# Two-bank PSUM tiles in the attention stages and a new sharing of the split steps in an attention and two-MLP kernel

## The chip, the cores and the metric

One core of one Trainium2 chip runs the whole program in one launch. The metric is the device time in microseconds (us) of one execution; a kernel's time is the median of several executions. The engines are TensorE (PE; PEld is its weight load), VectorE (DVE), ScalarE (ACT), GpSimd (POOL) and SyncE (SP), which issues most DMAs. Each runs its own instructions strictly in the order of its queue, and they wait for one another by semaphores.

## The reference, cut to what matters

For 4 batches of 12 heads with 448 positions of 64 elements:

```python
rmsnorm(x, g) = x / sqrt(mean(x*x) + 1e-6) * g
scores = (1/8) * rmsnorm(q, g_q) @ rmsnorm(k, g_k).T
attn   = exp(scores - max(scores)); attn /= sum(attn) + 1e-9
x = (attn @ v), heads side by side          # 1792 x 768
x = relu(x @ w_in)**2 @ w_out               # 768 -> 2048 -> 768
h = (x @ w1) * (x @ w2) @ w3                # 768 -> 1024 -> 1024
out = h @ wo2                               # 1024 -> 768
```

The MLP weights come as 64-bit floats, the rest as 32-bit floats.

## The kernel before, in words

**Precision.** TensorE works on fp32r operands. To keep fp32 accuracy each operand is cut into a high part (a rounded copy) and a low part (the value less the high part), and a product is three matmuls: high x high (L258), high weight x low activation (L259) and low weight x high activation (L260), the helper `mm3`.

**Weights.** They come in units of 128 x 384 or 128 x 512 (`units`), used in a fixed order. Units 0 to 31 are w3 and wo2, from which the kernel first makes w3 @ wo2 (`gen_w3o`, the stage called w3o below, U0 = 32). Units 32 to 119 are the MLP weights of batch 0 (U1 = 120). For both the 64-bit words are turned into fp32 on the chip: `words` (L192 on ACT for the high word, L195 on ACT or L197 on POOL for the low word, chosen by `LOW_ENG`), `join` (L204 on DVE), `split_hi` (L104 on ACT), `split_lo` (L112, on POOL or DVE by `LO0_ENG`). In the MLP of batch 0 the fp32 words are also stored; the batches 1 to 3 load those and only split them, with the low part always on POOL. There are four buffers each for the 64-bit unit (`raw64`), for the fp32 unit (`raw`) and for the split one (`hl`); the load of a unit is issued five units ahead, its words come three ahead, its join two and its high part one.

**Attention.** Heads run in a loop. Each head has stages: `head_prep` (k and q split; the high part of q, `qh`, at L487 on ACT or L489, by `QHI_ENG` with one letter for each batch), `stage_k` (k transposed, bank `kv`), `stage_qk` twice (two blocks of 112 rows each: L520 and L521 make scores in PSUM tile `sc`, L522 their negated maximum, L523 scales it), `stage_exp` (L538, two exponentials with sums), `stage_t` four times (L560 transposes the probabilities into PSUM tile `pt`, ACT copies it as the high part, `stage_lo` subtracts on DVE for the low part), `stage_v` (L609 into `kv`, then ACT and L617 add the halves into `xf`), and every second head `stage_x` (L598 transposes the inverse sums into `kv`, L623 multiplies `xf`, then it is split as the MLP's input).

**Order.** Between the stages `fill(n)` puts a share of the MLP matmuls of the batch before (of w3o in the first 12 heads). What the program gives is not quite the order on an engine: a planner lists the instructions of each engine beforehand by program order and by when it expects the operands, so matmuls of the fill can stand between those of a stage. PSUM has 8 banks: two `sc`, two `pt`, one `kv`, three `mm` for the fill.

Of the kernel before, what the change touches and what calls it, by code (L numbers as in the profile page):

```python
# [8 lines left out]
F32 = mybir.dt.float32  # L9
F32R = mybir.dt.float32r  # L10
# [4 lines left out]
ALU = mybir.AluOpType  # L15
AX = mybir.AxisListType
# [13 lines left out]
def attention_moe_kernel(  # L30
# [56 lines left out]
    t3 = ctx.enter_context(tc.tile_pool(name="t3", bufs=3))  # L87
    small = ctx.enter_context(tc.tile_pool(name="small", bufs=4))
    dram = ctx.enter_context(tc.tile_pool(name="dram", bufs=1, space=bass.MemoryType.DRAM))
    ps_sc = ctx.enter_context(tc.tile_pool(name="ps_sc", bufs=2, space=bass.MemoryType.PSUM))  # L90
    ps_pt = ctx.enter_context(tc.tile_pool(name="ps_pt", bufs=2, space=bass.MemoryType.PSUM))
    ps_kv = ctx.enter_context(tc.tile_pool(name="ps_kv", bufs=1, space=bass.MemoryType.PSUM))
    ps_mm = ctx.enter_context(tc.tile_pool(name="ps_mm", bufs=3, space=bass.MemoryType.PSUM))

# [221 lines left out]
    def gen_moe(b):  # L316
# [4 lines left out]
        for half in range(2):  # L321
            g = []

            def relu2(ps):
                r = t2.tile([128, S], F32, name="r", tag="r")
                nc.scalar.activation(out=r, in_=ps, func=AF.Relu)
                t = actp.tile([128, 2, S], F32R, name="act", tag="act")
                gf = t2.tile([128, S], F32, name="gf", tag="gf")
                nc.scalar.activation(out=t[:, 0, :], in_=r, func=AF.Square)
                nc.vector.tensor_tensor(out=gf, in0=ps, in1=r, op=ALU.mult)  # L330
                sub_on("g", t[:, 1, :], gf, t[:, 0, :].bitcast(F32))
                g.append(t)

            def keep(e):
# [174 lines left out]
    def stage_qk(h, s):  # L509
        if not (0 <= h < NH):  # L510
            return
        d = heads[h]
        nb = d["nb"] = small.tile([P, 2], F32, name="nb", tag="nb")
        c0 = 2 * s
        o = d["sc"] = [None, None]
        for j in range(2):
            c = c0 + j
            ps = ps_sc.tile([128, 512], F32, name="sc", tag="sc")
            o[j] = ps[:P, :S]
            nc.tensor.matmul(o[j], d["qh"][:, c * P:(c + 1) * P], d["kt"], start=True, stop=False)  # L520
            nc.tensor.matmul(o[j], d["ql"][:, c * P:(c + 1) * P], d["kt"], start=False, stop=True)  # L521
            nc.vector.tensor_reduce(out=nb[:, j:j + 1], in_=o[j], axis=AX.X, op=ALU.max, negate=True)  # L522
        nc.vector.tensor_tensor(out=nb, in0=nb, in1=d["rq"][:, c0:c0 + 2], op=ALU.mult)  # L523

    def stage_exp(h, s):
# [24 lines left out]
            )  # L550
            sums2[h // 2] = wide.rearrange("p c i d -> p c (i d)")

    def stage_t(h, kc):
        if not (0 <= h < NH):
            return
        d = heads[h]
        k0, kn = KCS[kc]
        ps = ps_pt.tile([128, 512], F32, name="pt", tag="pt")
        for c in range(C):
            nc.tensor.transpose(ps[:kn, c * P:(c + 1) * P], d["p"][c][:, k0:k0 + kn], ident)  # L560
        if kn == 128:
            t = t3.tile([128, 2, S], F32R, name="ptr", tag="ptr", bufs=3)
            hi, lo = t[:, 0, :], t[:, 1, :]
            d["pt"][kc] = [hi, lo]
        else:
            t = t1.tile([128, S], F32R, name="pte", tag="pte")
            hi, lo = t[:kn, :], t[kn:, :]
            d["pt"][kc] = [t]
        copy_on("a", hi, ps[:kn, :S])
        d["lo"].append((lo, ps[:kn, :S], hi.bitcast(F32)))  # L570
# [92 lines left out]
    for h in range(NH + 1):  # L663
# [91 lines left out]
```

## Time and profile before

| | us |
|---|---|
| median of 3 executions | 1255.01 (1254.23 to 1256.89) |
| the profiled execution | 1256.72 |
| its span, first to last instruction | 1254.9 |
| TensorE busy | 1176.6 |
| POOL busy | 788.5 |
| ACT busy | 749.0 |
| DVE busy | 692.6 |

The mean granted TensorE clock is 0.984 of full speed. Busy times are sums over the whole span; matmuls overlap one another in the record, so a busy TensorE need not be one at its peak. The stages differ: the attention of batch 0 with w3o comes first, then three batches of attention with the MLP of the batch before, and the last MLP alone.

### The profile page before, as it was taken

What the parts mean: (1) busy time and instruction counts of PE and PEld (TensorE: products, weight loads), DVE (VectorE), ACT (ScalarE), POOL (GpSimd) and SP (SyncE); (2) the same over time, 40 slices, a digit from 0 to 9 for tenths busy, and PEclk for the clock granted to TensorE, in tenths of its full rate; (3) what the DMA queues carried; (4) which work ended last, traced back from release to release, by engine and by line L of the source; (5) the groups of instructions that cost most, each with busy time, mean ns of one, the idle gap of its engine ahead of it and who ended that gap; (6) DMA issues with size and microseconds to landing.
All of it is one profiled execution on the core that took longest, in us unless ns stands there. A gap on an engine that the chain in (4) does not pass through costs nothing.

```text
span 1254.9 us, 18695 instructions
## 1 busy us (share of the span) xinstructions
PE 1176.6 (94%) x6192; PEld 1063.9 (85%) x6192; DVE 692.6 (55%) x1274; ACT 749.0 (60%) x1595; POOL 788.5 (63%) x770
## 2 busy tenths in 40 slices
PE   3789999798888999999999999999999999999998
PEld 2578888687777889999999998999999999999998
DVE  6699877666668676556557546555664431012100
ACT  5788877776755665665655555655545554443342
POOL 5874427746765555675876664765765656768773
PEclk9899999998998989999999999999999999999999
DMA  7774447866866754433334344333433333433342
GB/s 211 243 222 135 150 143 205 260 199 192 257 171 200 229 154 143 123 111 115 114 92 124 96 130 137 96 105 86 117 89 88 92 106 110 120 104 111 101 122 94
DMA packets 102129, 178.71 MB, mean 142 GB/s; under 512 B 11056, under 2 KB 65552, under 8 KB 102032
## 3 DMA queue, kind: packets, MB, share of 16 engines
q1 hardware_dynamic: 98576, 172.01, 46.9%
q10 hardware_dynamic: 3456, 5.51, 1.2%
q8 instruction: 49, 0.80, 0.3%
q14 instruction: 48, 0.39, 0.1%
HBM read 149.95 MB, written 27.53 MB: 141 GB/s over the span
## 4 chain that ended last, share of the span: by engine, by line
PE 65%; DVE 5%; DMA 4%; POOL 3%; ACT 2%; issue 2%; SPq 0%; POOLq 0%; DVEq 0%; ACTq 0%
PE mm L258 18%; PE mm L259 18%; PE mm L260 18%; PE pt L560 3%; PE kv L609 3%; DMA raw<-w 2%; DVE raw L204 2%; POOL hl L112 2%; PE sc L520 2%; PE sc L521 2%; DMA raw<-w_in 1%; DVE nb L522 1%; PE kv L504 1%; PE kv L598 1%; ACT p L538 0%
## 5 line engine op out<-in xcount | busy, mean ns | idle before, releaser
L112 POOL TENSOR_TENSOR hl<-raw,hl 128x384 fp32r<-128x384 f32 (+1 forms) x395 | 459.3, 1166 | 270.3 <-ACT hl L104 266.8
L104 ACT ACTIVATE hl<-raw 128x384 fp32r<-128x384 f32 (+1 forms) x416 | 234.0, 564 | 147.2 <-PE mm L260 79.3
L259 PE MATMUL mm<-x,hl 128*128 128x448 f32 (+1 forms) x832 | 307.3, 369 | 7.8 <-POOL x L112 7.8
L258 PE MATMUL mm<-x,hl 128*128 128x448 f32 (+1 forms) x832 | 311.9, 375 | 2.8 <-ACT x L104 1.8
L260 PE MATMUL mm<-x,hl 128*128 128x448 f32 (+1 forms) x832 | 306.3, 368 | 2.0 <-POOL hl L112 1.2
L258 PE MATMUL mm<-act,hl 128*128 128x448 f32 (+1 forms) x640 | 239.0, 373 | 0.0
L259 PE MATMUL mm<-act,hl 128*128 128x448 f32 (+1 forms) x640 | 235.7, 368 | 3.0 <-POOL act L112 2.9
L260 PE MATMUL mm<-act,hl 128*128 128x448 f32 (+1 forms) x640 | 234.6, 367 | 1.6 <-DVE hl L112 1.4
L538 ACT ACTIVATE p<-sc,nb,rr 112x448 f32<-112x448 f32 x192 | 137.5, 720 | 82.3 <-DVE nb L523 81.8
L259 PEld LDWEIGHTS mm<-x,hl 128*128 128x128 f32 x832 | 158.9, 191 | 21.7 <-POOL x L112 9.5
L258 PEld LDWEIGHTS mm<-x,hl 128*128 128x128 f32 x832 | 158.8, 191 | 17.4 <-ACT x L104 3.2
L260 PEld LDWEIGHTS mm<-x,hl 128*128 128x128 f32 x832 | 158.7, 191 | 16.3 <-POOL hl L112 2.3
L204 DVE SCALAR_TENSOR_TENSOR raw<-raw 128x384 uint32<-128x384 uint32 (+1 forms) x120 | 94.9, 794 | 77.0 <-POOL hl L112 66.3
L259 PEld LDWEIGHTS mm<-act,hl 128*128 128x128 f32 x640 | 121.9, 191 | 14.2 <-POOL act L112 4.6
L522 DVE TENSOR_REDUCE nb<-sc 112x1 f32<-112x448 f32 x192 | 113.3, 616 | 35.3 <-PE sc L521 34.0
L260 PEld LDWEIGHTS mm<-act,hl 128*128 128x128 f32 x640 | 121.8, 190 | 11.9 <-DVE hl L112 1.8
L112 POOL TENSOR_TENSOR act<-gf,act 128x448 fp32r<-128x448 f32 x96 | 117.5, 1225 | 22.0 <-DVE gf L330 8.5
L258 PEld LDWEIGHTS mm<-act,hl 128*128 128x128 f32 x640 | 122.2, 191 | 9.4
L112 DVE TENSOR_TENSOR ptr<-pt,ptr 128x448 fp32r<-128x448 f32 x144 | 86.8, 618 | 72.2 <-ACT ptr L104 72.0
L560 PE MATMUL pt<-ident,p 112*128 112x112 f32 (+1 forms) x768 | 101.0, 269 | 13.1 <-DVE ptr L112 10.3
L192 ACT ACTIVATE raw<-raw 128x384 f32<-128x384 f32 (+1 forms) x120 | 71.4, 598 | 57.9 <-DMA raw<-w 25.5
L560 PEld LDWEIGHTS pt<-ident,p 112*128 112x128 f32 (+1 forms) x768 | 82.5, 138 | 20.4 <-DVE ptr L112 10.9
(76 smaller groups left out, 1517.5 us busy)
## 6 DMA issues: line engine op xcount, KB each, us to landing
raw<-f_in SPq DMA_DIRECT2D x96, 192.0 KB, 2.4
raw<-f_out SPq DMA_DIRECT2D x72, 256.0 KB, 2.6
raw<-f SPq DMA_DIRECT2D x96, 192.0 KB, 2.4
raw<-w_in SPq DMA_DIRECT2D x32, 384.0 KB, 3.5
raw<-w_out SPq DMA_DIRECT2D x24, 512.0 KB, 4.2
raw<-w SPq DMA_DIRECT2D x32, 384.0 KB, 3.8
raw<-w3o SPq DMA_DIRECT2D x48, 256.0 KB, 2.7
qt<-q_t SPq DMA_DIRECT2D x48, 224.0 KB, 2.8
```

The source lines that it names most:

```text
L104: nc.scalar.activation(out=out, in_=in_, func=AF.Copy)
L112: e.tensor_tensor(out=out, in0=in0, in1=in1, op=ALU.subtract)
L192: nc.scalar.activation(out=hi, in_=hi, func=AF.Prelu, scale=2.0**-112, alpha=-(2.0**32))
L204: nc.vector.scalar_tensor_tensor(out=f[:, :n].bitcast(U32), in0=t[:, :n, 1], scalar=3, in1=t[:, :n, 0], op0=ALU.logical_shift_left, op1=AL ...
L258: nc.tensor.matmul(ps, w[:, 0, wk, :], x[0], start=(i == 0), stop=False)
L259: nc.tensor.matmul(ps, w[:, 0, wk, :], x[1], start=False, stop=False)
L260: nc.tensor.matmul(ps, w[:, 1, wk, :], x[0], start=False, stop=(i == last))
L520: nc.tensor.matmul(o[j], d["qh"][:, c * P:(c + 1) * P], d["kt"], start=True, stop=False)
L522: nc.vector.tensor_reduce(out=nb[:, j:j + 1], in_=o[j], axis=AX.X, op=ALU.max, negate=True)
L538: nc.scalar.activation(out=p, in_=o[j], func=AF.Exp, scale=d["rq"][:, c:c + 1], bias=nb[:, j:j + 1], accum_out=sm[:, i, c:c + 1],)
L560: nc.tensor.transpose(ps[:kn, c * P:(c + 1) * P], d["p"][c][:, k0:k0 + kn], ident)
L609: nc.tensor.matmul(ps[:, :S], w, m, start=(n == 0), stop=(n == len(ops) - 1))
```

## The change

1. **Scores.** `ps_sc` holds one tile of two banks in place of two tiles of one bank. Both blocks of a stage go into it, and one maximum over both banks replaces two.
2. **Transposes.** `ps_pt` holds one tile of two banks. `stage_t` runs twice for each head in place of four times: half 0 makes the first two key blocks (one copy and one subtraction over both banks), half 1 the third and the short fourth (a copy and a subtraction for each). The SBUF tile for the first two is one tile.
3. **Inverse sums.** `norms_to_rows` takes its bank from `ps_mm` (three) and not from `ps_kv` (one).
4. **Sharing.** The low words of units 0 to 31 are all on POOL (before, each third on ACT). The low parts of units 0 to 31 are all on POOL (before, each fifth on DVE); those of units 32 to 119 are on DVE for each third unit (before, each fifth). `qh` of the first 12 heads goes from ACT to POOL. In the MLP of batch 0 the subtraction after the squared relu goes from POOL to DVE (16 of them).

```diff
-    LO0_ENG = "ggggv"
+    LO0_ENG = "ggv"
-    QHI_ENG = "aavv"
+    QHI_ENG = "gavv"
-    ps_sc = ctx.enter_context(tc.tile_pool(name="ps_sc", bufs=2, space=bass.MemoryType.PSUM))
-    ps_pt = ctx.enter_context(tc.tile_pool(name="ps_pt", bufs=2, space=bass.MemoryType.PSUM))
+    ps_sc = ctx.enter_context(tc.tile_pool(name="ps_sc", bufs=1, space=bass.MemoryType.PSUM))
+    ps_pt = ctx.enter_context(tc.tile_pool(name="ps_pt", bufs=1, space=bass.MemoryType.PSUM))
-        if LOW_ENG[i % len(LOW_ENG)] == "a":
+        if i >= U0 and LOW_ENG[i % len(LOW_ENG)] == "a":
-        sub_on(LO0_ENG[i % len(LO0_ENG)] if i < U1 else "g", t[:, 1, :n], raws.pop(i)[:, :n], ...)
+        sub_on(LO0_ENG[i % len(LO0_ENG)] if U0 <= i < U1 else "g", t[:, 1, :n], raws.pop(i)[:, :n], ...)
-                sub_on("g", t[:, 1, :], gf, t[:, 0, :].bitcast(F32))
+                sub_on("g" if b else "v", t[:, 1, :], gf, t[:, 0, :].bitcast(F32))
 # stage_qk
+        ps = ps_sc.tile([128, 2, 512], F32, name="sc", tag="sc")
+        o = d["sc"] = [ps[:P, j, :S] for j in range(2)]
         for j in range(2):
...
-            nc.vector.tensor_reduce(out=nb[:, j:j + 1], in_=o[j], axis=AX.X, op=ALU.max, negate=True)
+        nc.vector.tensor_reduce(out=nb, in_=ps[:P, :, :S], axis=AX.X, op=ALU.max, negate=True)
 # stage_t(h, half)
+        ps = ps_pt.tile([128, 2, 512], F32, name="pt", tag="pt")
+        for j in range(2):
+            k0, kn = KCS[2 * half + j]
+            for c in range(C):
+                nc.tensor.transpose(ps[:kn, j, c * P:(c + 1) * P], d["p"][c][:, k0:k0 + kn], ident)
+        if half == 0:
+            t = t3.tile([128, 2, 2, S], F32R, name="ptr", tag="ptr0", bufs=1)
...
+            parts = [(t[:, 0], t[:, 1], ps[:, :, :S])]
+        else:
...
+            parts = [(t[:, 0, :], t[:, 1, :], ps[:, 0, :S]), (e[:kn, :], e[kn:, :], ps[:kn, 1, :S])]
+        for hi, lo, x in parts:
+            copy_on("a", hi, x)
+            d["lo"].append((lo, x, hi.bitcast(F32)))
 # norms_to_rows
-        ps = ps_kv.tile([128, 512], F32, name="kv", tag="kv")
+        ps = ps_mm.tile([128, 512], F32, name="mm", tag="mm")
 # the head loop: stage_t(h - 1, 0) and stage_t(h - 1, 1) take the places of the two pairs
```

## Rows read from the trace of the kernel before

**Rows 1.** Windows: stretch, length, busy PE, PEld, DVE, ACT, POOL, clock, DMA share, GB/s.

```profile
27.00:52.00 25.00, 14.95 (x53) 10.11 (x54) 16.07 (x27) 19.80 (x44) 21.29 (x22) 0.95 0.75 230
52.00:94.00 42.00, 36.39 (x210) 32.27 (x209) 38.14 (x68) 33.44 (x70) 32.04 (x34) 0.95 0.76 229
94.00:195.00 101.00, 94.91 (x581) 85.98 (x581) 85.63 (x184) 84.74 (x188) 41.84 (x54) 1.00 0.48 142
195.00:442.00 247.00, 214.22 (x1068) 188.05 (x1066) 168.19 (x295) 166.26 (x357) 156.22 (x160) 0.94 0.74 215
442.00:505.00 63.00, 62.11 (x324) 56.73 (x325) 46.83 (x77) 38.90 (x85) 36.08 (x34) 0.95 0.51 154
505.00:1045.00 540.00, 539.45 (x2917) 494.55 (x2916) 297.32 (x536) 308.06 (x670) 344.49 (x317) 1.00 0.37 107
```

**Rows 2.** Waits of TensorE, whole span: us in total, times, longest.

```profile
PE sc L520 <- ACT p L538: 17.4, 14, 2.9
PE kv L598 <- DVE xf L617: 13.4, 8, 4.2
PE pt L560 <- DVE ptr L112: 10.3, 6, 3.5
PE mm L259 <- POOL x L112: 7.8, 5, 2.9
...
PEld sc L520 <- ACT p L538: 26.8, 26, 3.3
```

**Rows 3.** Waits of all engines, 195 to 442 us.

```profile
DVE raw L204 <- POOL hl L112: 59.4, 35, 3.3
```

**Rows 4.** Chain that ended last, 405 to 416 us: start, us, what.

```profile
405.99 1.03 POOL hl L112
407.04 1.36 DVE raw L204
408.42 3.54 DMA raw<-w
...
413.98 1.03 POOL hl L112
415.04 0.57 DVE raw L204
```

**Rows 5.** Timeline: one scoring stage in w3o, TensorE.

```profile
145.65 0.46 PE L520 MATMUL sc<-kt,qh 128*112 128x448 f32 x1 [0.84 <-ACT p L538]
146.53 0.37 PE L520 MATMUL sc<-kt,qh 128*112 128x448 f32 x1
```

**Rows 6.** Timeline after 505 us: second exponential, next scores; subtractions, next transposes.

```profile
641.97 0.72 ACT L538 ACTIVATE p<-sc,nb,rr 112x448 f32<-112x448 f32 x1
646.55 0.36 PE L520 MATMUL sc<-kt,qh 128*112 128x448 f32 x1
588.89 1.16 DVE L112 TENSOR_TENSOR ptr<-pt,ptr 128x448 fp32r<-128x448 f32 x2 [2.03 <-ACT ptr L104]
590.32 0.96 PE L560 MATMUL pt<-ident,p 112*128 112x112 f32 x8
```

**Rows 7.** Groups by form: xcount | busy us, mean ns | idle before.

```profile
L522 DVE TENSOR_REDUCE nb<-sc 112x1 f32<-112x448 f32 x192 | 113.3, 616 | 35.3 <-PE sc L521 34.0
L448 DVE TENSOR_REDUCE ss<-qn 112x16 f32<-112x1024 f32 x22 | 26.7, 1214 | 7.2 <-ACT qn L446 7.1
L487 ACT ACTIVATE qh<-qt,gg 128x448 fp32r<-128x448 f32 x24 | 16.0, 667 | 1.5 <-PE sc L520 0.8 <-DMA qt<-q_t 0.8
```

**Rows 8.** Groups by form, POOL, 27 to 52 us.

```profile
L197 POOL TENSOR_SCALAR raw<-raw 128x384 uint32<-128x384 uint16 x10 | 8.1, 811 | 1.9 <-DMA raw<-wo 1.2
L112 POOL TENSOR_TENSOR act<-raw,act 128x384 fp32r<-128x384 f32 x6 | 7.0, 1164 | 1.3 <-ACT act L104 1.0
```

**Rows 9.** Groups by form, POOL, 195 to 505 us; then DVE, 195 to 442 us.

```profile
L112 POOL TENSOR_TENSOR hl<-raw,hl 128x384 fp32r<-128x384 f32 x48 | 50.8, 1064 | 24.3 <-ACT hl L104 23.3
L112 POOL TENSOR_TENSOR act<-gf,act 128x448 fp32r<-128x448 f32 x24 | 29.7, 1238 | 16.8 <-ACT act L104 6.4 <-DVE gf L330 6.2 <-ACT act L329 3.8
...
L112 DVE TENSOR_TENSOR ptr<-pt,ptr 128x448 fp32r<-128x448 f32 x27 | 16.1, 616 | 3.3 <-ACT ptr L104 3.3
L112 DVE TENSOR_TENSOR hl<-raw,hl 128x384 fp32r<-128x384 f32 x9 | 7.0, 775 | 0.0
```

More of the change, by code (lines that the diff above doesn't have):

```diff
@@ L228, in split_lo @@
         t = hls[i]
-        sub_on(LO0_ENG[i % len(LO0_ENG)] if i < U1 else "g", t[:, 1, :n], raws.pop(i)[:, :n], t[:, 0, :n].bitcast(F32))
+        sub_on(LO0_ENG[i % len(LO0_ENG)] if U0 <= i < U1 else "g", t[:, 1, :n], raws.pop(i)[:, :n], t[:, 0, :n].bitcast(F32))
     def upto(what, i, step):
@@ L514, in stage_qk @@
         c0 = 2 * s
-        o = d["sc"] = [None, None]
+        ps = ps_sc.tile([128, 2, 512], F32, name="sc", tag="sc")
+        o = d["sc"] = [ps[:P, j, :S] for j in range(2)]
         for j in range(2):
             c = c0 + j
-            ps = ps_sc.tile([128, 512], F32, name="sc", tag="sc")
-            o[j] = ps[:P, :S]
             nc.tensor.matmul(o[j], d["qh"][:, c * P:(c + 1) * P], d["kt"], start=True, stop=False)
             nc.tensor.matmul(o[j], d["ql"][:, c * P:(c + 1) * P], d["kt"], start=False, stop=True)
-            nc.vector.tensor_reduce(out=nb[:, j:j + 1], in_=o[j], axis=AX.X, op=ALU.max, negate=True)
+        nc.vector.tensor_reduce(out=nb, in_=ps[:P, :, :S], axis=AX.X, op=ALU.max, negate=True)
         nc.vector.tensor_tensor(out=nb, in0=nb, in1=d["rq"][:, c0:c0 + 2], op=ALU.mult)
@@ L551, in stage_exp, with stage_t @@
             sums2[h // 2] = wide.rearrange("p c i d -> p c (i d)")
-    def stage_t(h, kc):
+    def stage_t(h, half):
         if not (0 <= h < NH):
@@ L556, in stage_t @@
         d = heads[h]
[L557 to L564, printed above, removed]
-        else:
[L566 to L570, printed above, removed]
+        ps = ps_pt.tile([128, 2, 512], F32, name="pt", tag="pt")
[5 more added lines that the diff above has]
+            t = t3.tile([128, 2, 2, S], F32R, name="ptr", tag="ptr0", bufs=1)
+            d["pt"][0], d["pt"][1] = [t[:, 0, 0, :], t[:, 1, 0, :]], [t[:, 0, 1, :], t[:, 1, 1, :]]
+            parts = [(t[:, 0], t[:, 1], ps[:, :, :S])]
+        else:
+            t = t3.tile([128, 2, S], F32R, name="ptr", tag="ptr1", bufs=1)
+            d["pt"][2] = [t[:, 0, :], t[:, 1, :]]
+            e = t1.tile([128, S], F32R, name="pte", tag="pte")
+            d["pt"][3] = [e]
+            kn = KCS[3][1]
+            parts = [(t[:, 0, :], t[:, 1, :], ps[:, 0, :S]), (e[:kn, :], e[kn:, :], ps[:kn, 1, :S])]
+        for hi, lo, x in parts:
+            copy_on("a", hi, x)
+            d["lo"].append((lo, x, hi.bitcast(F32)))
     def stage_lo(h):
@@ L674, in attention_moe_kernel @@
         stage_t(h - 1, 0)
-        stage_t(h - 1, 1)
         fill(n)
@@ L681, in attention_moe_kernel @@
         stage_k(h + 1)
-        stage_t(h - 1, 2)
-        stage_t(h - 1, 3)
+        stage_t(h - 1, 1)
         fill(n)
```

## The prediction

> **What bounds the kernel now.** I read the windows first [rows 1]: stretch by stretch, what is not busy on TensorE is what a change off TensorE can win. From 505 us on TensorE is busy 539.45 of 540 us at full clock, so nothing there can come back. From 27 to 52 us it idles 10.0 of 25 us, from 52 to 94 us 5.6 of 42, from 94 to 195 us 6.1 of 101 and from 195 to 442 us, the MLP of batch 0, 32.8 of 247. In the last stretch the granted clock is 0.94; with levels of 1.2 and 2.4 GHz that is 12% of the stretch at the lower one, worth at most 0.06 x 247 = 14.8 us. So about 55 us of idling and 15 us of clock are in play, all before 442 us, and two thirds of it lie in the MLP of batch 0.
>
> The waits say what ends the idling [rows 2]. Scores wait for the exponentials that free their bank (17.4 us in 14 waits; the weight load, a step earlier, 26 times), the inverse sums for the `kv` bank to be read by L617 (13.4 us), transposes for the subtraction that frees `pt` (10.3 us), and in the first stage matmuls for the low part that POOL makes (7.8 us). Behind these stands a DVE that is itself held: from 195 to 442 us its join waits 59.4 us, 35 times, for POOL's subtraction to free an fp32 buffer [rows 3], and maxima, `xf` and `ptr` queue behind that join. The chain shows the circle [rows 4]: POOL's low part, the join, the load of a new unit into the buffer that the join frees (3.54 us), and 8.0 us after the first the next low part in the chain.
>
> **The change part by part.** The profiled execution took 1256.72 us (span 1254.9), 1.7 above the median of 1255.01; the sum is made against it, and the median's scale is 1.7 lower. No DMA is added or moved.
>
> *Fewer, longer instructions.* A maximum over 448 takes 616 ns and a reduction over 1024 takes 1214 [rows 7], 1.04 ns an element, so one over 896 is 1.08 us (estimate) against 1.23 for two. But two in a row already overlap: a pair of subtractions takes 1.16 us, not 1.23 [rows 6]. I cost the merging at 0 (from -0.15 us for each of 144 merged DVE pairs where DVE is the bound, some 75 of them before 505 us, so -11, to 0).
>
> *After 505 us.* The scores must now find both exponentials done. The second begins at 641.97 and takes 0.72 us, the scores start at 646.55 [rows 6]: almost 4 us of cover. The transposes have less: the two subtractions end at 590.05 and the transposes start at 590.32, a head with the group's sums; such a head comes every fourth. A two-bank copy can start only after both transposes, some 0.5 us late for the first bank. Cost 0, up to +3 if six such heads lose 0.5 us each.
>
> *One score tile (T2).* Before, the first block of the next scores waited for the first exponential alone; now for both. The price: first block 145.65, second 146.53 behind the next exponential, 0.88 us apart, and the fill between them [rows 5]. So the pair is pushed by up to 0.88 us in each of the 26 stages that wait [rows 2], 22.9 us at most; behind the late scores stand the fill on TensorE, and the maximum and the exponentials on DVE and ACT, for which the next scores wait. At the other end the planner lists the fill ahead of the pair and nothing is lost: 0. I take a quarter, +5.7: 14 of 26 waits now leave TensorE idle, and in w3o the 6.1 idle us of 101 say that fill is mostly at hand to go first.
>
> *One transpose tile (T3).* The second half now waits for both subtractions. Six waits exist [rows 2]; each grows by about half of the 1.16 us pair, 6 x 0.58 = +3.5 (0 to +5).
>
> *The inverse sums' bank (T4).* The wait for L617, 13.4 us, goes. Next late are the transposes and, through `kv`, `stage_k`, which needs the same L617 some 6 us of fill later. I count half, -6.7 (bounds -13.4 and +3, the latter if L623, now holding one of three `mm` banks, delays a product).
>
> *w3o, 27 to 52 us (T5).* POOL is busy 21.29 of 25 us [rows 1], and TensorE waits for its low parts. Added there: three low parts at 1.164, four low words and about two `qh` at 0.811 [rows 8], 3.5 + 3.2 + 1.6 = 8.3 us, against 3.7 us that POOL has free: +4.6. The 0.811 holds waiting too; I take +3.2 (0 to +8.3). `qh` on POOL waits for the q_t load, and the low parts queue behind it.
>
> *w3o, 52 to 195 us (T6).* DVE is busy 38.14 of 42 us and then 85% [rows 1]. It sheds three low parts, ACT about nine `qh` at 0.667 us [rows 7] and about five low words; POOL has room after 94 us (41.84 of 101). Of 11.7 idle us on TensorE I take -3 (from -11.7 to +5, the latter under the fourth rival).
>
> *MLP of batch 0 (T7).* Of its 88 units 30 low parts are on DVE, not 18: 12 leave POOL at 1.064 us, and 16 subtractions at 1.238 [rows 9]: 32.6 us of POOL's 156.2. DVE gains 12 x 0.775 and 16 at about 0.7 (between the two DVE rows there), 20.5 us, and goes from 68% to 76%. POOL makes 58 low parts in place of 70, 17% fewer of those for which the join waits [rows 3], and the rest no longer queue behind the 16. Of the idle time there that is not T4's (32.8 less 11.9, of the 13.4, in this stretch) I take 30%, -6.3. The clock follows the idle time: 40% of it gone less what T2 and T3 bring back leaves about 22% of 14.8, -3.2. T7 is -9.5; its bounds are -30 (all of both) and +7 (a third of DVE's new 20.5 us on the path).
>
> Sum: 5.7 + 3.5 - 6.7 + 3.2 - 3 - 9.5 = -6.8, 1249.9 on the profiled execution's scale and 1248 on the median's.
>
> **The rivals.**
>
> *The score tile decides (slower).* If the planner has no fill to put ahead, the 26 stages lose the full 0.88: 17.2 us over the forecast, and the 3.2 us of clock do not come back: +13.6. On the median's scale 1268.6 at the full price, 1258 at two thirds of it; I give 1264. It overtakes the gains from 12.5 us on, 0.48 for each stage. For it: from 94 to 195 us ACT and DVE are both about 84% busy, so a stage's loop of maximum and exponentials has little slack. Against: those engines shed work there.
>
> *The circle keeps the pace (no change).* If load, join and low part go on at 8 us a turn [rows 4], the next wait takes over and T7 is 0: +2.7, 1257.7. For it: 3.54 us of the turn is the load, which nothing shortens.
>
> *The lock-step breaks (much faster).* T4 whole and T7 twice: -23, 1232. For it: one late join explains most stalls of the stretch.
>
> *POOL and DVE hold each other up.* Of two like joins one takes 1.36 us, right behind one POOL subtraction, and one 0.57 [rows 4]. Moving 22 steps from ACT to POOL before 195 us makes more such meetings: T5 8.3 and T6 +5, in sum +6, 1261. The Trainium skill, "SBUF — State Buffer", section "Who interferes with whom", says that a DVE instruction with two SBUF inputs contends with GpSimd's reads, that whichever issues first blocks the other, and that ACT never waits on anyone. By that rule the move off ACT costs more than the moved times; the two joins agree with it. It also speaks for T7, where POOL gets emptier.
>
> **How the numbers follow.** Forecast 0.47, the score tile 0.18, the circle 0.15, the broken lock-step 0.13, POOL against DVE 0.07. The forecast's own range is 1241 to 1255. The range 1231 to 1265 reaches into the rivals and leaves out about 2 in 10: the full price of the score tile above, more than twice the gain of T7 below. A change under 0.2% (2.5 us) can't be told from none. Faster: 0.43 + 0.13 + 0.02 of the circle = 0.58. Same: 0.03 + 0.07 + 0.02 = 0.12. Slower: 0.30, nearly all of the score tile and of POOL, and a part of the circle.
>
> **What would show it.** T4: no wait of L598 for L617. T2: the waits of L520 for L538 grow by less than 6 us over the span; if by over 12, the first rival. T5: TensorE reaches the end of the first 20 units 3 to 4 us later. T7: the join's wait for POOL falls from 59.4 to below 45 us, the clock rises above 0.96, and the stretch that begins at 195 us ends some 12 us sooner after its start. After 505 us TensorE stays without gaps; gaps at transposes there would prove the cost of 0 wrong.

## The result, and the profile after

The prediction was a gain of 6.8 us; the change costs about 16.

| | before | after |
|---|---|---|
| median, us | 1255.95 (1254.23 to 1258.34) | 1272.66 (1270.97 to 1274.57) |
| ratio | 1 | 1.0131, 95% interval 1.0112 to 1.0150 |
| span of the profiled execution, us | 1254.9 | 1269.2 |

The windows of the kernel after, in the columns of [rows 1], and its waits of TensorE over the whole span, as in [rows 2]:

```profile
27.00:52.00 25.00, 14.21 (x37) 9.44 (x37) 16.30 (x27) 14.00 (x31) 22.51 (x26) 1.00 0.53 162
52.00:94.00 42.00, 33.67 (x157) 28.84 (x158) 25.42 (x37) 26.79 (x56) 35.71 (x38) 0.88 0.65 199
94.00:195.00 101.00, 90.95 (x548) 81.11 (x547) 78.52 (x136) 73.91 (x157) 48.73 (x64) 0.98 0.49 142
195.00:442.00 247.00, 218.58 (x1105) 195.51 (x1104) 183.35 (x314) 171.67 (x360) 128.54 (x133) 0.94 0.71 215
...
505.00:1045.00 540.00, 539.22 (x2924) 494.60 (x2923) 312.54 (x480) 309.94 (x654) 340.56 (x320) 1.00 0.38 108
```

```profile
PE pt L561 <- DVE ptr L112: 17.2, 9, 3.9
...
PE sc L519 <- ACT p L537: 11.2, 7, 3.2
...
PE kv L614 <- DVE ptr L112: 9.9, 5, 3.9
...
PE mm L259 <- POOL x L112: 7.2, 5, 3.3
```

From 505 us on nothing changed for TensorE. From 52 to 195 us ACT and DVE have less to do than in [rows 1] (from 52 to 94 us DVE 25.42 for 38.14, ACT 26.79 for 33.44), yet TensorE also does less: the work comes late. POOL alone is fuller up to 195 us: 22.51 of 25, 35.71 of 42 and 48.73 of 101 us.

Fixed windows mislead once the work has shifted, so I followed the units of weights. Each of the 120 units of 64-bit words is joined once, by DVE at L204; the joins in order of time are a clock of the work. Below are the 20th, the 46th and the 120th join (the last of batch 0's MLP): start, us, what; first of the kernel before, then of the kernel after.

```profile
58.92 0.68 DVE L204 SCALAR_TENSOR_TENSOR raw<-raw 128x512 uint32<-128x512 uint32 x1
...
210.84 1.49 DVE L204 SCALAR_TENSOR_TENSOR raw<-raw 128x384 uint32<-128x384 uint32 x1
...
458.61 0.54 DVE L204 SCALAR_TENSOR_TENSOR raw<-raw 128x384 uint32<-128x384 uint32 x1
```

```profile
67.83 0.69 DVE L204 SCALAR_TENSOR_TENSOR raw<-raw 128x512 uint32<-128x512 uint32 x1 [0.52 <-POOL raw L197]
...
231.97 0.55 DVE L204 SCALAR_TENSOR_TENSOR raw<-raw 128x384 uint32<-128x384 uint32 x1
...
473.96 0.54 DVE L204 SCALAR_TENSOR_TENSOR raw<-raw 128x384 uint32<-128x384 uint32 x1
```

The 20th join is 8.9 us late, the 46th 21.1, the 120th 15.4; from there to the end the kernel after takes 1.1 us less. So by the 46th join w3o loses 21 us and the MLP of batch 0 gives 5.8 back; how far this mark can be trusted is said under the table below.

What w3o waits for: the waits of all engines for POOL's low word, from 27 to 195 us, in the kernel after. Before the change the like wait was 2.6 us, all of it before the 20th join.

```profile
DVE raw L204 <- POOL raw L197: 18.2, 15, 2.6
```

### The profile page after: what moved, and what is told of

It reads as the page before. It is cut to its first block, busy times and chain, and to the rows that moved or that the text cites. A ratio compares the mean times of both kernels' runs of the same rounds, so it can differ in the third digit from the quotient of the medians.

```text
span 1269.2 us, 18630 instructions
## 1 busy us (share of the span) xinstructions
PE 1183.7 (93%) x6192; PEld 1070.5 (84%) x6192; DVE 702.9 (55%) x1152; ACT 736.3 (58%) x1525; POOL 773.3 (61%) x770
## 4 chain that ended last, share of the span: by engine, by line
PE 62%; DVE 2%; DMA 1%; ACT 1%; issue 1%; POOL 0%; SPq 0%; ACTq 0%; POOLq 0%
PE mm L258 17%; PE mm L259 17%; PE mm L260 17%; PE pt L561 3%; PE kv L614 3%; PE sc L520 2%; PE sc L519 2%; DMA raw<-w 1%; PE kv L504 1%; PE mm L603 0%; DVE raw L204 0%; DVE nt L429 0%; POOL hl L112 0%; ACT p L537 0%; DVE ptr L112 0%
## 5 line engine op out<-in xcount | busy, mean ns | idle before, releaser
L112 POOL TENSOR_TENSOR hl<-raw,hl 128x384 fp32r<-128x384 f32 (+1 forms) x386 | 443.2, 1152 | 276.6 <-ACT hl L104 274.1
L258 PE MATMUL mm<-act,hl 128*128 128x448 f32 (+1 forms) x640 | 241.7, 378 | 2.2 <-ACT acc L104 1.5
L259 PE MATMUL mm<-act,hl 128*128 128x448 f32 (+1 forms) x640 | 238.4, 372 | 5.3 <-POOL act L112 2.7
L260 PE MATMUL mm<-act,hl 128*128 128x448 f32 (+1 forms) x640 | 237.0, 370 | 2.1 <-POOL hl L112 2.1
L260 PEld LDWEIGHTS mm<-x,hl 128*128 128x128 f32 x832 | 157.9, 190 | 14.6 <-POOL hl L112 1.6
L259 PEld LDWEIGHTS mm<-act,hl 128*128 128x128 f32 x640 | 123.5, 193 | 17.1 <-POOL act L112 7.7
L258 PEld LDWEIGHTS mm<-act,hl 128*128 128x128 f32 x640 | 123.9, 194 | 13.1 <-ACT acc L104 1.8
L260 PEld LDWEIGHTS mm<-act,hl 128*128 128x128 f32 x640 | 123.7, 193 | 12.5 <-POOL hl L112 2.8
L112 DVE TENSOR_TENSOR ptr<-pt,ptr 128x896 fp32r<-128x896 f32 x96 | 82.0, 854 | 92.8 <-ACT ptr L104 67.9
L204 DVE SCALAR_TENSOR_TENSOR raw<-raw 128x384 uint32<-128x384 uint32 (+1 forms) x120 | 89.3, 750 | 77.5 <-POOL hl L112 51.4
L561 PE MATMUL pt<-ident,p 112*128 112x112 f32 (+1 forms) x768 | 100.3, 270 | 23.3 <-DVE ptr L112 17.2
L197 POOL TENSOR_SCALAR raw<-raw 128x384 uint32<-128x384 uint16 (+1 forms) x90 | 68.9, 766 | 73.4 <-DMA raw<-w_in 30.9
L521 DVE TENSOR_REDUCE nb<-sc 112x2 f32<-112x896 f32 x96 | 104.0, 1084 | 13.1 <-PE sc L520 12.3
L561 PEld LDWEIGHTS pt<-ident,p 112*128 112x128 f32 (+1 forms) x768 | 82.0, 138 | 31.8 <-DVE ptr L112 16.5
```

Source lines behind the costliest of these rows:

```text
L197: nc.gpsimd.tensor_scalar(out=t[:, :n, 0], in0=low, scalar1=2.0**-13, scalar2=2.0**-14 - 0.5, op0=ALU.mult, op1=ALU.add)
L204: nc.vector.scalar_tensor_tensor(out=f[:, :n].bitcast(U32), in0=t[:, :n, 1], scalar=3, in1=t[:, :n, 0], op0=ALU.logical_shift_left, op1=AL ...
L258: nc.tensor.matmul(ps, w[:, 0, wk, :], x[0], start=(i == 0), stop=False)
L259: nc.tensor.matmul(ps, w[:, 0, wk, :], x[1], start=False, stop=False)
L260: nc.tensor.matmul(ps, w[:, 1, wk, :], x[0], start=False, stop=(i == last))
L521: nc.vector.tensor_reduce(out=nb, in_=ps[:P, :, :S], axis=AX.X, op=ALU.max, negate=True)
```

## The experiments

Every ratio is to the kernel before in runs on the same chip; 0.001 is 1.26 us. The last four columns are from one profiled execution each: how much later than in the kernel before the 20th join starts, how much longer the 20th to the 120th and the rest then take, and the span. One execution can differ from the ratio by some us: that of e13 adds up to 3.2 us for a ratio of 6.7. (Between the 20th and the 120th I don't split: where the 46th falls varies by 10 us among versions that share w3o as before, and is given back; in e1 it is 8.3 us late without any loss at the 120th.)

| run | ratio, 95% interval | to 20th | 20th to 120th | rest | span |
|---|---|---|---|---|---|
| after | 1.0131 (1.0112 to 1.0150) | +8.9 | +6.4 | -1.1 | 1269.2 |
| e1_share_back | 0.9989 (0.9980 to 0.9999) | -0.1 | +0.2 | -1.1 | 1254.0 |
| e2_one_bank | 1.0053 (1.0037 to 1.0070) | +7.8 | +1.4 | -1.7 | 1262.5 |
| e3_neither | 0.9949 (0.9934 to 0.9964) | -0.6 | -2.6 | -0.6 | 1251.1 |
| e4_only_w3o_share | 1.0125 (1.0109 to 1.0140) | +7.1 | +9.3 | +0.2 | 1271.5 |
| e5_qh_only | 1.0091 (1.0066 to 1.0117) | +0.7 | +9.0 | -0.3 | 1264.3 |
| e6_low_only | 1.0093 (1.0070 to 1.0116) | +6.4 | +6.0 | -0.5 | 1266.9 |
| e7_lo_only | 1.0026 (1.0012 to 1.0040) | +1.1 | +2.3 | +0.1 | 1258.4 |
| e8_nb_scalar | 1.0059 (1.0039 to 1.0080) | +9.7 | -1.4 | -1.0 | 1262.2 |
| e9_sc_only | 0.9973 (0.9961 to 0.9984) | +2.6 | -4.9 | +0.6 | 1253.2 |
| e10_pt_only | 0.9972 (0.9959 to 0.9984) | -2.2 | -0.7 | +0.4 | 1252.4 |
| e11_best_nb | 0.9951 (0.9933 to 0.9969) | +0.3 | -1.1 | -1.8 | 1252.3 |
| e12_bank_only | 1.0022 (1.0013 to 1.0032) | -0.4 | +6.6 | -1.5 | 1259.6 |
| e13_qh_dve | 1.0053 (1.0033 to 1.0072) | +0.7 | +2.9 | -0.4 | 1258.1 |
| e14_control | 1.0026 (1.0014 to 1.0038) | -1.3 | +2.7 | +2.2 | 1258.6 |
| e15_qh_both | 1.0028 (1.0014 to 1.0041) | +1.9 | +3.1 | -2.6 | 1257.4 |
| e16_mlp_share | 0.9957 (0.9944 to 0.9969) | -0.7 | -4.4 | -0.3 | 1249.6 |
| e17_pool_time | 1.0231 (1.0212 to 1.0250) | +31.5 | +2.4 | -3.2 | 1285.7 |
| e18_half | 0.9903 (0.9883 to 0.9923) | +1.8 | -11.6 | +0.6 | 1245.8 |

### Which part costs: four kernels

e1 is the kernel after with the w3o sharing undone, e2 with one-bank tiles, e3 with both undone; e4 is the kernel before with the w3o sharing alone.

```diff
# e1 (and e3), against after
-        if i >= U0 and LOW_ENG[i % len(LOW_ENG)] == "a":
+        if LOW_ENG[i % len(LOW_ENG)] == "a":
-        sub_on(LO0_ENG[i % len(LO0_ENG)] if U0 <= i < U1 else "g", ...)
+        sub_on("ggggv"[i % 5] if i < U0 else LO0_ENG[i % len(LO0_ENG)] if i < U1 else "g", ...)
-    QHI_ENG = "gavv"
+    QHI_ENG = "aavv"
# e2 (and e3), against after: stage_qk and stage_t as before
-    ps_sc = ctx.enter_context(tc.tile_pool(name="ps_sc", bufs=1, ...))
+    ps_sc = ctx.enter_context(tc.tile_pool(name="ps_sc", bufs=2, ...))
-    ps_pt = ctx.enter_context(tc.tile_pool(name="ps_pt", bufs=1, ...))
+    ps_pt = ctx.enter_context(tc.tile_pool(name="ps_pt", bufs=2, ...))
# e4, against before: only the w3o lines of the change
```

> The changed kernel with the sharing of the w3o stage put back (low words of units 0 to 31 on ACT each third, low parts on DVE each fifth, qh of batch 0 on ACT); two-bank tiles, the mm bank and the sharing of the MLP of batch 0 stay. In the changed trace all of the loss is there before 235 us (+23 at the 13th head) and 9 us come back after. Theory A, POOL overloaded in w3o costs about 9 to 12 us of it: about 1262, and the value matmuls of head 0 come at about 39 us, not 47.7. Theory B, the two-bank tiles cost it all: about 1271, head 12 still at +20 us. Theory C, the planner's order scatters the time by 5 to 10 us whatever is edited: anything, and the four runs of this call don't add up.

> The changed kernel with one-bank score and transpose tiles again (all four stages as before); the new sharing and the mm bank stay. Theory A (POOL in w3o): about 1264, head 0 still at 47 us, heads 2 to 12 in w3o at the former period of about 11.4 us. Theory B (two-bank tiles): about 1248, head 0 back near 40 us. Theory C: does not add up with the other runs.

> The kernel before with only the mm bank for the inverse sums and the new sharing of the MLP of batch 0 (units 32 to 119 each third low part on DVE, 16 subtractions after the squared relu on DVE); w3o sharing and one-bank tiles as before. Theories A and B alike: w3o as before (head 12 within 2 us of 211), the MLP of batch 0 shorter by 9 us as in the changed kernel: about 1247. If it comes out at 1255 or more, the 9 us that the changed kernel won back after 235 us belong to the two-bank tiles or only to its late start.

> The kernel before with only the new sharing of the w3o stage (28 more steps on POOL before 195 us), all else as before. Theory A: +9 to +12, about 1266, head 0 at 47 us. Theory B: within 3 us of the kernel before. With e1 it tells whether the sharing costs the same with and without the two-bank tiles.

The sharing in w3o costs 15.7 us alone (e4), 13.1 with the rest of the change but the tiles (e2 less e3) and 17.8 with the whole of it (after less e1). The tiles cost 5.0 (e1 less e3) or 9.8 (after less e2). The rest gains 6.4 (e3). The three add up to the result within some 2 us: 15.7 + 5.0 - 6.4 = 14.3, against 16.5. The loss is thus shown to be the sharing's, and it is larger than either theory gave it (9 to 12 us, or at most 3).

### The three moves of the sharing, one at a time

```diff
# e5
-    QHI_ENG = "aavv"
+    QHI_ENG = "gavv"
# e6
-        if LOW_ENG[i % len(LOW_ENG)] == "a":
+        if i >= U0 and LOW_ENG[i % len(LOW_ENG)] == "a":
# e7
-        sub_on(LO0_ENG[i % len(LO0_ENG)] if i < U1 else "g", ...)
+        sub_on(LO0_ENG[i % len(LO0_ENG)] if U0 <= i < U1 else "g", ...)
```

> The kernel before with one edit: qh of the first 12 heads on POOL, not ACT. The whole w3o sharing alone cost +16 us, of which head 0 was +15 late but head 1 only +2.7, and then about +1.3 us a head to head 10. Theory A1 (POOL is late with qh: the planner lists ql before the scaled maximum on DVE, so ql's wait for qh holds the exponentials and the next scores; seen once in full at 119 to 124 us of that trace): +6 to +9 us, growing by about 0.8 us a head from head 2 on. Theory A2 (POOL is overloaded only in the first 20 units): 0 to +2.

> The kernel before with one edit: the low words of units 0 to 31 all on POOL. In the trace of the whole w3o sharing DVE's join waits 19.0 us for POOL's low words from 27 to 195 us, in the kernel before 2.6. Theory A1: +4 to +6, most of it by head 2, the join's wait for L197 rises from 2.6 to 10 or more. Theory A2 (POOL's load in the first stage is all): +10 or more. Rival: ACT, 0.55 us lighter for each of ten low words, gives it back: 0.

> The kernel before with one edit: the low parts of units 0 to 31 all on POOL (six move from DVE). Theory A1: +2 to +4, in the first 20 units. Theory A2: +5. Rival: DVE is the fuller engine from 52 to 94 us and sheds 4 us: 0 or a gain of 2. If e5, e6 and e7 add up to much less than 16, the three edits cost through POOL's total load and not each by itself.

They cost 11.4, 11.7 and 3.3 us, in sum 26 for a whole of 16, and in different places: the low words 6.4 us before the 20th join, `qh` nearly all of it after. Expected by the first theory were 6 to 9, 4 to 6 and 2 to 4 us, so only e7 fell within it. Up to the 20th join POOL tells the story. The windows from 12 us to that join, in the columns of [rows 1]; kernel before, then the sharing alone (e4), then the low words alone (e6):

```profile
12.00:58.92 46.92, 28.95 (x103) 20.61 (x103) 31.66 (x67) 31.91 (x70) 37.14 (x40) 0.93 0.74 233
```

```profile
12.00:66.00 54.00, 32.89 (x115) 24.17 (x115) 31.20 (x68) 30.85 (x66) 44.59 (x53) 0.81 0.65 193
```

```profile
12.00:65.37 53.37, 30.41 (x105) 22.19 (x106) 37.86 (x82) 31.65 (x68) 44.03 (x50) 0.87 0.63 199
```

POOL's busy time is the fifth busy column. In e4 it does 7.45 us more and the join comes 7.1 later; in e6 6.89 more, and 6.4 later. Its idle time hardly shrinks, 9.4 and 9.3 us of the stretch for 9.8 before. Most of it are waits for loads and for steps of ACT and DVE, which the added steps did not fill; the longest in the kernel before, from 12 to 58.92 us:

```profile
POOL raw L197 <- DMA raw<-wo: 3.3, 2, 2.1
POOL hl L112 <- ACT hl L104: 1.5, 1, 1.5
```

The wait that carries the loss is the join's, in e4 from 12 to 66 us (2.6 us before the change):

```profile
DVE raw L204 <- POOL raw L197: 16.0, 12, 1.9
```

For the time after the 20th join, the timeline of e5 shows one place out of the 9.0 us. `ql`, which needs POOL's `qh`, stands ahead of the scaled maximum on DVE, and the words of an MLP unit stand ahead of the exponentials on ACT. Their load had come by 126.68 us; the scaled maximum was there at 126.77 us, and the exponentials began 0.8 us later:

```profile
126.03 0.68 DVE L492 SCALAR_TENSOR_TENSOR ql<-qt,gg,qh 128x448 fp32r<-128x448 f32 x1
...
126.62 0.15 DVE L523 TENSOR_TENSOR nb<-nb,rr 112x2 f32<-112x2 f32 x1
126.68 0.57 ACT L192 ACTIVATE raw<-raw 128x384 f32<-128x384 f32 x1 [3.46 <-DMA raw<-w_in]
...
127.59 0.72 ACT L538 ACTIVATE p<-sc,nb,rr 112x448 f32<-112x448 f32 x1
...
128.54 0.43 PE L520 MATMUL sc<-kt,qh 128*112 128x448 f32 x1 [1.30 <-ACT p L538]
```

and e4 shows another, where `ql` waits for POOL's `qh` ahead of the scaled maximum on DVE:

```profile
119.97 1.14 DVE L492 SCALAR_TENSOR_TENSOR ql<-qt,gg,qh 128x448 fp32r<-128x448 f32 x1 [0.99 <-POOL qh L489]
...
121.03 1.78 DVE L523 TENSOR_TENSOR nb<-nb,rr 112x2 f32<-112x2 f32 x1
...
121.54 1.26 POOL L112 TENSOR_TENSOR hl<-raw,hl 128x512 fp32r<-128x512 f32 x1
...
122.85 0.72 ACT L538 ACTIVATE p<-sc,nb,rr 112x448 f32<-112x448 f32 x1 [3.15 <-DVE nb L523]
...
123.81 0.43 PE L520 MATMUL sc<-kt,qh 128*112 128x448 f32 x1 [3.16 <-ACT p L538]
```

Neither place is a full engine; in each, steps in front of the scoring loop come late. In e4 the late `qh` is 0.99 us of it; the larger part is that `ql` took 1.14 us for a usual 0.67 and the scaling 1.78 for a usual 0.15, while POOL worked (see the last section). In e4 the scores wait for the exponentials from 66 to 226 us (20th to 46th join), where the like wait was 5.8 us:

```profile
PE sc L520 <- ACT p L538: 14.6, 10, 3.2
```

This wait, from the 20th join to the 46th, tells the kernels apart: 10.7 us in e5, 9.3 in e6 and 14.6 in e2, but 3.7 to 6.8 in every other kernel with score tiles of one bank (5.4 to 6.0 in e13 and e15 of the next section). In the kernel after it is 0.5, and the value matmuls wait 9.9 us instead. So the loss after the 20th join passes through the scoring loop where `qh` or the low words are all made on POOL; how it divides between late operands and other lists is not shown.

### POOL's time or the way over POOL

e13 takes `qh` off ACT without POOL; e15 gives POOL a copy of that work that nothing reads; e17 gives it extra work for all three moves on a constant; e14 adds one tiny instruction.

```diff
# e13
-    QHI_ENG = "aavv"
+    QHI_ENG = "vavv"
# e14, head loop
+        if h == 2:
+            nc.gpsimd.memset(t1.tile([P, 2], F32, name="idle", tag="idle"), 0.0)
# e15, head_prep, first 12 heads; qh itself stays on ACT
+                idle = t1.tile([128, 112], mybir.dt.bfloat16, name="idle", tag="idle")
+                for c0 in range(0, S, 112):
+                    nc.gpsimd.tensor_scalar(
+                        out=idle, in0=qt[:, c0:c0 + 112], scalar1=gg[:, 0:1], scalar2=1.0, op0=ALU.mult, op1=ALU.mult)
# e17: four of these for each step that the sharing would move
+            if two:
+                nc.gpsimd.tensor_tensor(out=t[:P, :n], in0=ident[:, :n], in1=ident[:, P - n:], op=ALU.subtract)
+            else:
+                nc.gpsimd.tensor_scalar(out=t[:P, :n], in0=ident[:, :n], scalar1=1.0, scalar2=1.0, ...)
```

> The kernel before with qh of the first 12 heads on DVE in place of ACT; POOL keeps its work. Theory A and B (POOL): most of the 11.4 us that qh on POOL cost is gone; DVE is the busier engine of the two, so a loss of 0 to 5 us stays, ratio 1.000 to 1.004. Theory C (another order after any edit, or ACT's list without qh): about the same loss as with qh on POOL, ratio 1.006 to 1.010.

> The kernel before with one more instruction: POOL clears 2 elements a partition in one head of batch 0; nothing reads them. It changes the planner's lists and no work. Theory A and B: ratio 0.999 to 1.001. Theory C: the time moves by several us in either direction, outside 0.998 to 1.002, and then part of what the other experiments showed is a matter of the lists.

> The kernel before with a second copy of qh's product for the first 12 heads on POOL, in four pieces, that nothing reads; qh itself stays on ACT. POOL gets at least the time that qh on POOL took, about 1 us a head, and no operand comes over it. Theory A (POOL's time): 6 to 14 us slower, ratio 1.005 to 1.011. Theory B (the way over POOL): ratio 0.999 to 1.003.

> The kernel before, with POOL doing at least as much extra work in w3o as the new sharing gives it (four short instructions on a constant for each low word, low part and qh that the sharing would move), which nothing reads; all operands are made where they were. Theory A (POOL's time, and DVE held up by its reads): ratio 1.008 to 1.013. Theory B (the operands' way over POOL): ratio 1.000 to 1.005, as with the qh copy alone.

e17 lost far more than either theory said. Its extra instructions, in the groups by form of POOL from 12 to 94 us (xcount | busy us, mean ns | idle before), and its window to the 20th join:

```profile
L196 POOL TENSOR_SCALAR idle<-ident 112x112 bf16<-112x112 f32 x43 | 15.1, 351 | 3.0
...
L196 POOL TENSOR_SCALAR idle<-ident 112x102 bf16<-112x102 f32 x20 | 7.0, 348 | 1.5
...
L196 POOL TENSOR_SCALAR idle<-ident 112x76 bf16<-112x76 f32 x20 | 6.3, 315 | 1.1
...
L194 POOL TENSOR_TENSOR idle<-ident 112x102 bf16<-112x102 f32 x12 | 5.6, 470 | 0.8
...
L194 POOL TENSOR_TENSOR idle<-ident 112x76 bf16<-112x76 f32 x12 | 4.2, 349 | 0.9
```

```profile
12.00:90.43 78.43, 34.01 (x103) 24.71 (x103) 29.25 (x65) 31.74 (x70) 69.57 (x147) 1.00 0.45 141
```

They read only a constant, so the planner can list them early: 38.2 us of them lie before 94 us. That is more than the sharing adds to POOL (e4 has 120.98 us busy from 12 to 195 us, the kernel before 105.79), which is why the loss is larger. POOL is busy 32.4 us more up to the 20th join, and that join is 31.5 us late; after it, with them gone, 2.4 us are lost to the 120th. Up to that join no wait of POOL is left: the 8.9 us in which it is not busy are gaps between its 147 instructions. So a queue of POOL that never waits is the path up to the 20th join, at 0.97 us lost for each us added, though nothing reads the results: theory A for work that is listed early. The copies of e15 have to wait for `qt`, and lie elsewhere:

```profile
12.00:60.83 48.83, 30.22 (x103) 21.40 (x103) 29.01 (x66) 32.03 (x70) 43.66 (x56) 0.90 0.71 228
60.83:215.80 154.97, 142.44 (x848) 128.53 (x849) 134.73 (x269) 127.10 (x276) 92.02 (x124) 0.99 0.55 162
```

Here 6.5 us of extra POOL time cost 1.9, since they went into POOL's waits (5.2 us idle, not 9.8). After the 20th join POOL has 92 of 155 us busy, 11 us more than before (80.97 of 151.92), for 3 us. So after the 20th join POOL's time is nearly free, and the 9.0 us that `qh` on POOL costs there are not its time: that speaks for theory B, the way of the operands, and for the lists that follow. But `qh` on DVE, with nothing over POOL, still costs 6.7 us in the ratio (2.9 there in its one execution), between what theories A and B (0 to 5) and theory C, another order (about 8 to 13), gave it; so of the 11.4 us of e5 some 5 at most can be put down to POOL, and the intervals of e5 and e13 touch. And e14, whose edit does no work, costs 0.26%, outside what theories A and B allowed and as theory C said: a new list alone can cost that much. Of parts that cost 0.3% or less (e7, e15, the bank of e12, each two-bank tile) the cause can't be separated from a new list, and one such control doesn't say how much more a list can do.

### The parts with a small effect

```diff
# e9, against e3: the two-bank score tile alone; e10: the two-bank transpose tile alone (as in the change)
# e12, against before: only the bank of the inverse sums
-        ps = ps_kv.tile([128, 512], F32, name="kv", tag="kv")
+        ps = ps_mm.tile([128, 512], F32, name="mm", tag="mm")
# e8 against after, e11 against e3: the product that scales the maxima, as two with one tensor from SBUF each
-        nc.vector.tensor_tensor(out=nb, in0=nb, in1=d["rq"][:, c0:c0 + 2], op=ALU.mult)
+        for j in range(2):
+            nc.vector.tensor_scalar(out=nb[:, j:j + 1], in0=nb[:, j:j + 1],
+                scalar1=d["rq"][:, c0 + j:c0 + j + 1], scalar2=None, op0=ALU.mult)
```

> The kernel before with the mm bank, the new sharing of the MLP of batch 0 and the two-bank score tile with its one maximum (transposes and w3o sharing as before). Without the score tile that is 1251.8 beside 1257.5 (ratio 0.995); with both two-bank tiles 1256.4 (0.999). Theory of the prediction (the score tile costs up to 0.88 us in each stage that waits): ratio 0.999 or more, waits of L519 for the exponentials up. Rival (in the changed kernel's trace these waits nearly vanish in w3o, and value matmuls wait for the subtraction instead, so the transpose tile is what costs): ratio 0.995 to 0.996.

> The same base with the two-bank transpose tile alone, scores in two one-bank tiles. Theory of the prediction (+3.5 us): ratio 0.997 to 0.998. Rival (the transpose tile is what costs): 0.999 or more, with waits of the value matmul for the ptr subtraction and of the transposes that come back.

> The kernel before with one edit: the inverse sums take a bank of the fill's three. Prediction: of 13.4 us of waiting half comes back as the next wait, -6.7 us, ratio 0.995. Rival 1: all of it goes, 0.989. Rival 2: the next wait (transposes, exponentials behind the same late DVE) takes all, 1.000, and the 0.995 of this with the new sharing of the MLP belongs to the sharing.

> The changed kernel, but the scaling of the maximum (a product of two 112x2 SBUF tiles) is done as two multiplications by a scalar for each partition, one tensor input each. In every trace here the long ones of these (over 0.25 us, up to 1.8 against 0.15) end when a POOL instruction ends, 16 of 48 before 505 us. Theory D (DVE is locked out by POOL when it reads two SBUF tiles, and this stands on the way from scores to exponentials): no long one left, 4 to 8 us faster than the changed kernel, 1265 to 1268. Rival: the lock only moves to the next DVE instruction with two SBUF inputs, within 2 us of 1272.

> The kernel before with the mm bank, the new sharing of the MLP of batch 0 and the scaling of the maximum by two multiplications by a scalar (one tensor input each). On the changed kernel that last edit gained 9 us (ratio 1.0131 to 1.0059). Theory D (the lock of DVE by POOL on the way from scores to exponentials costs this everywhere before 505 us): 4 to 9 us under the same kernel without it, ratio 0.988 to 0.992. Rival (there it helped only because POOL was full in w3o): 0.994 to 0.996.

The score tile costs 3.0 us on e3 and the transpose tile 2.9, of the size of e14. Each lengthens the wait that the prediction named, by 2 us over the span; first e3, then e9 for the scores, then e3 and e10 for the transposes:

```profile
PE sc L520 <- ACT p L538: 15.7, 16, 2.7
```

```profile
PE sc L519 <- ACT p L537: 17.9, 11, 3.0
```

```profile
PE pt L560 <- DVE ptr L112: 14.7, 12, 3.0
```

```profile
PE pt L562 <- DVE ptr L112: 16.8, 11, 4.1
```

The bank costs 2.8 alone, also of the size of e14. The waits of TensorE in e12 from 195 to 445 us show why it gains nothing:

```profile
PE pt L560 <- DVE ptr L112: 15.7, 7, 4.6
...
PE mm L258 <- DVE gf L330: 4.8, 1, 4.8
...
PE mm L258 <- ACT acc L104: 3.0, 1, 3.0
```

The wait of L598 for L617 (11.9 us there before) is gone, but the transposes wait 15.7 us (9.2 before), and 7.8 us are new: products that wait for a free `mm` bank. e8 gains 9.0 us on the kernel after, and e11 nothing on e3. Both agree with what was expected of the long products of the maxima: that they cost time in the kernel after (4 to 8 us), and that they do so only because POOL is full there. Against it, the change did not lengthen them: before 505 us the kernel before has 14 of over 0.25 us and the kernel after 16, 10.0 and 9.5 us in sum above the usual 0.15; from the 20th join to the 46th the kernel after has four of over 0.6 us, 3.5 us in all. Its value matmuls (9.9 us) wait only 3.4 in e8. I take a part of e8 for another list, which is not shown; then a list alone can move more than e14 did.

### The part that gains

```diff
# e16, against before
-    LO0_ENG = "ggggv"
+    LO0_ENG = "ggv"
-        sub_on(LO0_ENG[i % len(LO0_ENG)] if i < U1 else "g", ...)
+        sub_on("ggggv"[i % 5] if i < U0 else LO0_ENG[i % len(LO0_ENG)] if i < U1 else "g", ...)
-                sub_on("g", t[:, 1, :], gf, t[:, 0, :].bitcast(F32))
+                sub_on("g" if b else "v", t[:, 1, :], gf, t[:, 0, :].bitcast(F32))
# e18, against e16
-    LO0_ENG = "ggv"
+    LO0_ENG = "gv"
```

> The kernel before with the new sharing in the MLP of batch 0 alone (each third low part of units 32 to 119 on DVE, the 16 subtractions after the squared relu on DVE); tiles, banks and w3o as before. By difference of two runs (with the mm bank 0.9949, the mm bank alone 1.0022) it should be 0.9927, 9 us faster, if the two parts add up; theory C, or if the two parts share a gain: 0.995 to 1.000.

> As the sharing in the MLP of batch 0 alone, with each second low part of units 32 to 119 on DVE in place of each third (44 in place of 30). If POOL's queue of low parts is what the join waits for: up to 3 us faster again, ratio 0.992 to 0.996. If DVE, at 182 of 247 us there, is by now the busier of the two: ratio 0.997 to 1.002.

e16 gains 5.4 us, e18 12.2: it beats before and after. The windows from 195 to 442 us and the join's wait in them, first of e16, then of e18 ([rows 1] and [rows 3] for the kernel before):

```profile
195.00:442.00 247.00, 215.16 (x1090) 189.26 (x1089) 181.56 (x327) 170.47 (x367) 133.17 (x138) 0.96 0.74 221
```

```profile
DVE raw L204 <- POOL hl L112: 46.1, 26, 3.6
```

```profile
195.00:442.00 247.00, 224.73 (x1131) 197.85 (x1131) 191.70 (x355) 176.01 (x378) 118.56 (x130) 0.95 0.76 227
```

```profile
DVE raw L204 <- POOL hl L112: 40.2, 23, 4.0
```

The wait falls from 59.4 over 46.1 to 40.2 us as low parts leave POOL, and the 20th to the 120th join take 4.4 and 11.6 us less, although DVE goes from 168 to 192 us busy. e16 gained less than the 9 us that e3 and e12 gave by difference. The gain in e18 exceeded the 3 us expected: DVE at 78% was not yet the bound.

## Why the prediction was wrong, point by point

**T5 and T6, the sharing in w3o, failed; the sign of the result is theirs.** The prediction had +3.2 and -3; the sharing alone measured +15.7 (e4). T5 let 3.7 us "that POOL has free" pay for a part of the added 8.3. That idle time was mostly POOL waiting for loads and for ACT and DVE: in e4 and e6 it stayed, and the 20th join came later by nearly what POOL got, 7.1 us for 7.45. e17 shows that POOL's queue alone can set that join (31.5 us for 32.4), e15 that work which falls into the waits costs less (1.9 for 6.5). The value 3.2 should have stood at its upper bound; "3 to 4 us later" for the first 20 units was 8.9 in the kernel after, read at the 20th join. T6 gave a credit for what DVE and ACT shed. They did shed it, and it won nothing: after the 20th join the sharing cost another 4 to 9 us (after less e1 6.2, e2 less e3 4.0, e4 9.3), through the scoring loop, whose wait rose from 5.8 to 14.6 us in e4. That this comes from operands made late on POOL is argued from two places of the timeline, not shown. T6's bound of +5 was too narrow, as I bounded by POOL's room and not by its order. With 15.7 for T5 and T6, nothing for T4, 5.0 for T2 and T3 and -5.4 for T7 the sum is +15.3, against 16.5 measured.

**T4 failed: no gain.** -6.7 predicted, +2.8 measured (e12), which is no more than e14 cost. The wait of L598 went, as said. In its place came the upper bound's reason, products that wait for a free `mm` bank (7.8 us), and 6.5 us more at the transposes. On top of the new sharing it cost nothing (e3 against e16: 0.9949 and 0.9957).

**T2 and T3 came near in sum, partly by luck.** 9.2 predicted, 5.0 measured without the w3o sharing and 9.8 with it. Alone, T2 measured 3.0 for 5.7 and T3 2.9 for 3.5, by the waits that they named (e9, e10). In the kernel after these waits shifted: that of the scores fell from 17.4 [rows 2] to 11.2 us, that of the transposes rose from 10.3 to 17.2, and the value matmuls wait 9.9 us for the subtraction (3.1 in e1), a wait that T3 did not have.

**Nothing after 505 us was right, and merging at 0 fits.** No run has the merging without the two-bank tiles. The merged maximum and subtraction, by form in the kernel after:

```profile
L521 DVE TENSOR_REDUCE nb<-sc 112x2 f32<-112x896 f32 x96 | 104.0, 1084 | 13.1 <-PE sc L520 12.3
...
L112 DVE TENSOR_TENSOR ptr<-pt,ptr 128x896 fp32r<-128x896 f32 x48 | 52.3, 1089 | 68.0 <-ACT ptr L104 67.9
```

1084 ns is the 1.08 us estimated; a pair of subtractions went from 1.16 [rows 6] to 1.09 us.

**T7 was right in sign and mechanism, and over-sized.** -9.5 predicted, -5.4 measured alone (e16), of which 4.4 us lie between the 20th and the 120th join. The join's wait fell as expected; in the kernel after, from 195 to 442 us:

```profile
DVE raw L204 <- POOL hl L112: 39.4, 23, 3.6
```

The clock did not rise there (0.94; 0.96 in e16), and with it went most of the 3.2 us counted for it. "Some 12 us sooner" was 5.8 from the 46th to the 120th join of the kernel after, by the mark that moves among versions, and T4 had no part in it.

**The rivals.** The score tile as the bound falls, though its 1264 to 1268.6 were nearest in time: e9 cost 3.0. (Its "1258 at two thirds" leaves out the 3.2 us of clock that the full price counts; with them it is 1261.) The circle that keeps its pace falls, since e16 and e18 shorten it; the broken lock-step too. POOL against DVE (1261) named the right terms, T5 and T6, with a chance of only 0.07, but its mechanism did not grow. Joins and scaled maxima, both with two inputs from SBUF, take no longer in e4 than in the kernel before. Before, then e4, over the whole span:

```profile
L204 DVE SCALAR_TENSOR_TENSOR raw<-raw 128x384 uint32<-128x384 uint32 (+1 forms) x120 | 94.9, 794 | 77.0 <-POOL hl L112 66.3 <-DMA f_in<-raw 3.1 <-POOL raw L197 2.6
...
L523 DVE TENSOR_TENSOR nb<-nb,rr 112x2 f32<-112x2 f32 x96 | 31.7, 331 | 1.1
```

```profile
L204 DVE SCALAR_TENSOR_TENSOR raw<-raw 128x384 uint32<-128x384 uint32 (+1 forms) x120 | 93.2, 778 | 92.4 <-POOL hl L112 71.0 <-POOL raw L197 19.0 <-DMA f_out<-raw 1.2
...
L523 DVE TENSOR_TENSOR nb<-nb,rr 112x2 f32<-112x2 f32 x96 | 30.6, 319 | 1.0
```

Why the three moves together cost less than their sum, and how the loss after the 20th join divides between late operands, long products in the wrong place (e8) and new lists, stays open.

## What to carry to other kernels

An engine with idle time has room only if the added work can run in its waits: look at what each idle stretch waits for before it pays for anything. Here POOL, 79% busy up to the 20th join, gave 7.1 us of delay for 7.45 us of work in its way, and 1.9 for 6.5 us that fell into its waits. Before clearing a busy engine, ask whose operands will come late in front of the tightest loop, and follow the work by a mark that each unit passes once (here the join), not by fixed windows. Among experiments on small parts, run one edit that does no work: a difference of its size (here 0.26%) means nothing, and several such edits would say how far a larger one can be trusted.

## What the runs showed of the hardware

A product of 112 x 2 elements on DVE took 1.78 us in e4 where 0.15 us is usual; it ended at 122.81, as POOL's subtraction from 121.54 did at 122.80. The same holds elsewhere: in the kernel after, 31 such products take over 0.25 us, and each ends within 0.03 us of the end of an instruction of POOL. The Trainium skill, "SBUF — State Buffer", section "Who interferes with whom", has a DVE instruction with two SBUF inputs contend with a GpSimd instruction that reads SBUF, and the traces agree. What it costs the whole kernel differs: with the two inputs taken away no product takes over 0.22 us, and the time fell by 9.0 us in one kernel (e8) and did not change in another (e11).
